# Retention and a squared-ReLU feed-forward in one kernel: q loaded in two DMAs over all partitions, its head groups mixed, and the clusters of small matmuls joined from the fifth group on

## The chip, the cores and the metric

The kernel runs on one core of a Trainium2 chip. Its time is the device time of one execution in microseconds, the median of several runs. A profile is one more execution, recorded by the hardware profiler; its span, 288.5 us here, is counted from the first to the last instruction and is a little shorter than the run's time.

## The reference

Two stages follow each other. The first is retention, attention without a softmax: per head, scores are masked by a decay that falls with distance.

```
scores = (q @ k^T) / sqrt(64)                      # q, k, v: 8 batches, 8 heads, 576 tokens, 64 wide
Dmat   = gamma_h ** (i - j) for i >= j, else 0     # gamma_h = 1 - 2^(-5 - h)
attn   = (scores * Dmat) @ v
x      = attn as (batch, token) rows of 8 x 64 = 512 columns      # 4608 x 512
out    = (relu(x @ w_in) ** 2) @ w_out             # w_in 512 x 2048, w_out 2048 x 512, fp32
```

## The kernel before

**Tiling.** The 4608 tokens are 36 units of 128 tokens: 32 "full" units (a batch, a chunk of 128 tokens) and 4 "tail" units that hold the last 64 tokens of two batches. Two units are a group, so there are 18 groups, numbered from 0 (the fifth is group 4). Retention is done chunk by chunk with a running state R (a 64 x 64 sum of k times v per head, decayed from chunk to chunk); a chunk's output is its own masked scores times v, plus q times the state of the chunks before. The decays are folded into v, into the state and into the output (`gam_full`), so the mask is zeros and ones.

**Where q and k come from.** Both are needed with the 64 columns of a head on the partitions, so they are cast to fp16 and transposed.
- Units 0 to 7 (`PAIRED = 8`) are loaded two at a time, 512 KB each for k, q and v (`add_load_pair`, line 308; the DMA is line 316): a partition holds two neighbouring tokens of every head, in packets of 2 x 64 x 4 = 512 bytes. Casts (line 424, v with its decay line 420) go to VectorE, ScalarE or GpSimd as line 411 says; TensorE transposes (line 439) into a PSUM tile `psT`, and four copies (line 450) bring it to `kqT`. Scores, masks (`mask2`, line 490), state sums and outputs of such a pair are written by `add_ret_pair`; its output becomes `xT` in line 577.
- Units from 8 on are loaded one at a time (`add_load`, line 290). k and v come in packets of 256 bytes, one token of one head. q comes in packets of 1 KB, four tokens of one head, in four DMAs (lines 297 to 299), each to 32 partitions: partition 32 x + r holds tokens 4 r to 4 r + 3 of heads x and 4 + x. GpSimd casts (lines 371, 382, 387) and SyncE's DMA transpose (line 400) makes `kqT`. There the columns of head group x are 32 x to 32 x + 31, so `qT` (line 607) hands the matmuls four runs of 16 neighbouring columns.

**Weights.** w_in and w_out come in four pieces each, issued from GpSimd (line 331), which casts them to fp16 on the way. The first waits for the first v; k of unit 4 waits for the sixth piece (line 318). w_in is used by `ph` (line 876), w_out and four difference matrices wT (line 827) by `po` (lines 916 and 973: from group 1 on the second product is a Strassen scheme with sums gS, line 946).

**Clusters.** Retention's matmuls are 64 x 64 "quads", four at a time on the array, all on line 357. For units from 8 on they stand in clusters: scores and state sums of a group (`fa`, line 778), and its outputs (`fb`, line 809). From the group `JOIN` on, they are joined: `f1` (line 790) is the state part of group g's outputs with group g+1's scores, `f2` (line 794) is group g+1's sums with the rest of g's outputs.

**What sets the order.** Every engine's program is written by a planner (`Schedule`, lines 16 to 100) at build time. A task has an engine, a key (the lowest key of the ready ones goes first), an estimated duration, dependences and buffers that it takes. The planner plays the estimates through and emits the instructions in that order; on the chip each engine then runs its list in order and waits where data are late. Loads, transposes and stores are all on SyncE's list. Junk matmuls (line 256, `WARM = 34` of them) have the last key and fill TensorE's start. VectorE tasks have fixed durations in the planner, whether GpSimd works beside them or not.

Of the kernel before, what the change touches and what calls it, by code (L numbers as in the profile page):

```python
# [15 lines left out]
class Schedule:  # L16
# [6 lines left out]

    def add(self, eng, key, dur, fn, deps=(), acq=(), after=None, lag=0.0):
        t = dict(eng=eng, key=key, dur=dur, fn=fn, acq=acq, n=len(self.tasks), users=[], free=[], lag=lag,
                 left=len(deps), ready=0.0, lat=self.LAT[eng] if after is None else after)
        for d in deps:
            d["users"].append(t)
        self.tasks.append(t)
        return t  # L30
# [11 lines left out]
    def emit(self):  # L42
# [13 lines left out]
        now = 0.0  # L56
        while True:
            for e in ready:
                if busy[e]:
                    continue  # L60
                held = []
                while ready[e]:
                    item = heapq.heappop(ready[e])
                    t = item[2]
                    if all(self.count[r] >= t["acq"].count(r) for r in t["acq"]):
                        for r in t["acq"]:
                            self.count[r] -= 1
                        t["start"] = now
                        order.append(t)
                        busy[e] = True  # L70
                        push(now + t["dur"], "end", t)
                        break
                    held.append(item)
                for item in held:
                    heapq.heappush(ready[e], item)
            if not events:
                break
            now = events[0][0]
            while events and events[0][0] <= now + 1e-9:
                _, _, what, t = heapq.heappop(events)  # L80
                if what == "end":
                    busy[t["eng"]] = False
                    for w in t["users"]:

                        push(now + (0.0 if w["eng"] == t["eng"] else t["lat"]), "dep", w)
                    for g in t["free"]:
                        push(now + t["lat"], "free", g)
                elif what == "dep":
                    t["left"] -= 1
                    if t["left"] == 0:  # L90
                        push(now + t["lag"], "go", t)
                elif what == "go":
                    heapq.heappush(ready[t["eng"]], (t["key"], t["n"], t))
                else:
                    t["left"] -= 1
                    if t["left"] == 0:
                        self.count[t["res"]] += 1
# [6 lines left out]
def kernel(  # L104
# [105 lines left out]

    mask2 = const.tile([P, 2, 2, 64], FP32, name="mask2")
    nc.gpsimd.memset(mask2, 1.0)
    for c in range(2):
        for e in range(2):
            m = mask2[c * 64:(c + 1) * 64, e]
            nc.gpsimd.affine_select(out=m, in_=m, compare_op=ALU.is_ge, fill=0.0, base=-e, pattern=[[1, 2], [2, 64]],  # L216
                                    channel_multiplier=-2)
# [17 lines left out]
    SQ_LATE = (1, 4, 6)  # L235
    JOIN = 5
    LAG = {"k4": 0.7, "q4": 0.5}
    LAG_T, LAG_O = 1.5, 5.0
# [51 lines left out]
    def add_load(u):  # L290
        kind, b, c = units[u]
        for n, (name, src) in enumerate((("k", k), ("q", q), ("v", v))):
            def fn(name=name, src=src):
                x = ld.tile([P, H, D], FP32, name=f"{name}32", tag=f"{name}32")
                tile_of[name + "32", u] = x
                if kind == "full" and name == "q":
                    for j in range(NP):
                        nc.sync.dma_start(out=x[32 * j:32 * j + 32].rearrange("r (a t) d -> r a (t d)", a=2),
                                          in_=src[b, :, c * P:(c + 1) * P, :].rearrange("(a x) (r t) d -> x r a (t d)", a=2, t=4)[j])
                elif kind == "full":  # L300
# [7 lines left out]
    def add_load_pair(name, u):  # L308
        n = "kqv".index(name)

        def fn():
# [91 lines left out]
    def add_unit_pair(u, base):  # L403
# [4 lines left out]
        for i, name in enumerate("kqv"):  # L408
            xs[name] = []
            for e in range(2):  # L410
                eng = ("DVE" if (e if name == "v" else lead) else "ACT" if name == "k" and u >= 4 or u == 2 and e else
                       "DVE" if name == "q" and u == 2 else "POOL")

                def fc(name=name, e=e, eng=eng):
# [4 lines left out]
                    if name == "v":  # L419
                        (nc.vector if eng == "DVE" else nc.gpsimd).tensor_tensor(  # L420
                            out=t.rearrange("p (h d) -> p h d", d=D), in0=x,
                            in1=vdec[f"pair{e}"].rearrange("p (h o) -> p h o", o=1).to_broadcast([P, H, D]), op=ALU.mult)
                    else:
                        engines[eng](out=t.rearrange("p (n b a d) -> p n b a d", n=2, b=2, a=2),
# [9 lines left out]
        for i, name in enumerate("kq"):  # L434
# [9 lines left out]
            for s in range(2):  # L444
                on_act = i == 0 or s == 0 or u > 0

                def fe(i=i, s=s, on_act=on_act):
                    if i == 0:
                        tile_of["kqT", u + s] = work.tile([P, 2 * NP, P], FP16, name="kqT", tag="kqT", bufs=6)
                    (nc.scalar.copy if on_act else nc.vector.tensor_copy)(  # L450
                        out=tile_of["kqT", u + s][:, i * NP:(i + 1) * NP].rearrange("p x (e t) -> p e x t", e=2),
                        in_=tile_of["psT", u, i][:, :, :, half(s)])
                es.append(add("ACT" if on_act else "DVE", base + 3 + i + s / 2, 0.66, fe, deps=[t] + T["kqT", u + s],
# [14 lines left out]
    def add_ret_pair(g):  # L468
# [7 lines left out]
        for e in range(2):  # L476
# [11 lines left out]
            for a in range(2):  # L488
                def fm(e=e, a=a):
                    nc.vector.tensor_tensor(  # L490
                        out=rT[e][:, a], in0=rT["ps", e][a].rearrange("p (n i) -> p n i", i=P),
                        in1=mask2[:, e].rearrange("p (o e) i -> p o (e i)", o=1).to_broadcast([P, NP, P]), op=ALU.mult)
                ms.append(add("DVE", base + 5 + e, 0.66, fm, deps=[t] + ms))
# [79 lines left out]
        for s in range(2):  # L573
            def fx(s=s):
                if s == 0:
                    tile_of["x", g] = x_pool.tile([P, NP, 2 * P], FP16, name="xT", tag="xT")
                nc.vector.tensor_tensor(
                    out=tile_of["x", g][:, :, s * P:(s + 1) * P].rearrange("p n (i e) -> p n e i", e=2),
                    in0=tile_of["psO", g][s].rearrange("p (n e i) -> p n e i", n=NP, e=2),
                    in1=gam_f.rearrange("p n (i e) -> p n e i", e=2), op=ALU.mult)  # L580
            T["x", u + s] = add("DVE", base + 25 + s, 0.7, fx, deps=[t] + ([T["x", u]] if s else []), acq=() if s else ("x",))
# [119 lines left out]
    def after_sums(g, t, key, res):  # L701
# [23 lines left out]
        r1 = add("DVE", key + 0.2 - URGENT, 0.69, fr1, deps=[r0])  # L725
        r2 = add("DVE", key + 0.3, 0.65, fr2, deps=[r1], acq=("R",))
        T["Rm", g], T["R", g], T["Rread", g], T["Rmread", g] = r0, r2, [], r1
# [94 lines left out]
    def add_wT(i, in0, in1):  # L822
        ts = []
        for h in range(2):
            def f(h=h):
                sl = slice(h * HF // 2, (h + 1) * HF // 2)
                nc.vector.tensor_tensor(out=wT[i][:, sl], in0=in0[:, sl], in1=in1[:, sl], op=ALU.subtract)
            ts.append(add("DVE", WT_KEY + i, 0.7, f, deps=sum((wcast[j] for j in range(4, 8 if i else 6)), [])))
        return ts
# [5 lines left out]
    for x, y in ((t2, t1), (t4, t2)):  # L835
        for p in y:
            for w in x:
                sched.need(w, p)
    wT_done = {7: t3, 6: t2, 5: t1, 4: t4}
# [18 lines left out]
    def add_ff(g):  # L858
# [10 lines left out]
        for fb in range(NF // nf):  # L869
# [18 lines left out]
            def fg(fb=fb, on_act=on_act):  # L888
# [43 lines left out]
    def add_strassen(g, us, base, sq):  # L932
# [179 lines left out]
```

## Time and profile before

| what | value |
|---|---|
| time, median of 3 runs | 289.84 us (289.72 to 289.88) |
| span of the profiled run | 288.5 us |
| TensorE busy | 280.7 us, 97% of the span |
| ScalarE busy | 187.5 us, 65% |
| VectorE busy | 177.7 us, 62% |
| GpSimd busy | 87.1 us, 30% |
| ph, line 876 | 1152 matmuls, 136.6 us |
| q loads of units from 8 on | 96 DMAs of 64 KB, median 3.2 us to landing |
| q loads of units 0 to 7 | 4 DMAs of 512 KB, median 6.1 us to landing |

How to read it: a busy TensorE is one with a matmul in its pipeline, so a matmul's listed 273 ns is its latency; a run of 256-column ones goes in one each 109 ns (64 in 6.99 us on the chain of work). The time of a stretch of matmuls is therefore read from the start of one group to the start of the next. Junk matmuls count as busy too. In a time line, brackets at the end of a row hold the idle time of that engine before the row and what ended it. The chain of work that ended last goes back from the last instruction to whatever released it; TensorE has 88% of it, and DMA 3%.

### The profile page before, as it was taken

What the parts mean: (1) busy time and instruction counts of PE and PEld (TensorE: products, weight loads), DVE (VectorE), ACT (ScalarE), POOL (GpSimd) and SP (SyncE); (2) the same over time, 40 slices, a digit from 0 to 9 for tenths busy, and PEclk for the clock granted to TensorE, in tenths of its full rate; (3) what the DMA queues carried; (4) which work ended last, traced back from release to release, by engine and by line L of the source; (5) the groups of instructions that cost most, each with busy time, mean ns of one, the idle gap of its engine ahead of it and who ended that gap; (6) DMA issues with size and microseconds to landing.
All of it is one profiled execution on the core that took longest, in us unless ns stands there. A gap on an engine that the chain in (4) does not pass through costs nothing.

```text
span 288.5 us, 10135 instructions
## 1 busy us (share of the span) xinstructions
PE 280.7 (97%) x4346; PEld 236.0 (82%) x4346; DVE 177.7 (62%) x341; ACT 187.5 (65%) x363; POOL 87.1 (30%) x124
## 2 busy tenths in 40 slices
PE   7999999999999999999999999999999999999994
PEld 2568767888888888888888888888888888888883
DVE  3772389868466756657666574767666566364632
ACT  5558975667584757667575748675848665847830
POOL 5660045433525243423325151534433100000000
PEclk9999999999999999999999999999999999999999
DMA  7999999999999898989898997989899420102004
GB/s 202 275 208 206 248 277 267 168 240 144 212 222 186 210 201 216 179 214 168 222 146 197 231 185 182 220 200 248 177 160 228 110 75 5 73 2 75 0 2 145
DMA packets 122156, 49.94 MB, mean 173 GB/s; under 512 B 94720, under 2 KB 117760, under 8 KB 122112
## 3 DMA queue, kind: packets, MB, share of 16 engines
q1 hardware_dynamic: 117568, 44.84, 71.0%
q0 software_dynamic: 4224, 4.19, 8.8%
q8 instruction: 34, 0.56, 0.8%
q10 hardware_dynamic: 320, 0.26, 0.4%
q14 instruction: 10, 0.08, 0.1%
HBM read 36.70 MB, written 9.44 MB: 160 GB/s over the span
## 4 chain that ended last, share of the span: by engine, by line
PE 88%; DMA 3%; DVE 3%; POOL 2%; issue 2%; DVEq 0%; POOLq 0%
PE ph L876 43%; PE po L973 36%; PE psO L357 4%; DMA w_in<-in_moe_w_in_dram 3%; PE po L916 2%; PE psS L357 2%; PE psc L357 2%; DVE rx L490 1%; DVE o L996 1%; DVE gS L946 1%; POOL mask L216 0%; DVE vx L420 0%; POOL vx L420 0%; POOL w_in L331 0%; PE psT L439 0%
## 5 line engine op out<-in xcount | busy, mean ns | idle before, releaser
L876 PE MATMUL ph<-xT,w_in 128*128 128x256 f16 x1152 | 136.6, 273 | 0.3 <-DMA w_in<-in_moe_w_in_dram 0.3
L876 PEld LDWEIGHTS <-w_in 128*128 128x128 f16 x1152 | 111.4, 98 | 14.7 <-DMA w_in<-in_moe_w_in_dram 0.6
L884 ACT ACTIVATE rl<-ph 128x512 f16<-128x512 f32 x144 | 84.3, 586 | 50.7 <-PE ph L876 48.1
L894 ACT ACTIVATE gT<-rl 128x512 f16<-128x512 f16 x118 | 74.4, 631 | 3.4
L973 PEld LDWEIGHTS <-gS 128*128 128x128 f16 x544 | 51.7, 98 | 6.5
L973 PE MATMUL po<-wT,gS 128*128 128x256 f16 x408 | 55.8, 273 | 0.0
L946 DVE TENSOR_TENSOR gS<-gT,gS 128x512 f16<-128x512 f16 (+1 forms) x51 | 31.3, 613 | 24.2 <-ACT gT L894 23.7
L973 PEld LDWEIGHTS <-gT 128*128 128x128 f16 x408 | 39.6, 98 | 4.8
L973 PE MATMUL po<-w_out,gT 128*128 128x256 f16 x272 | 36.8, 273 | 0.0
L387 POOL TENSOR_TENSOR v<-v,vdec_full 128x512 f16<-128x512 f32 x24 | 26.6, 1108 | 28.1 <-DMA v<-in_v_dram 24.4
L371 POOL CAST kq<-k 128x512 f16<-128x512 f32 x28 | 19.7, 702 | 36.9 <-DMA k<-in_k_dram 31.2
L946 DVE TENSOR_TENSOR gS<-gT 128x1024 f16<-128x1024 f16 x34 | 24.7, 726 | 6.4 <-ACT gT L894 6.3
L382 POOL CAST kq<-q 128x512 f16<-128x512 f32 x24 | 15.6, 649 | 32.0 <-DMA q<-in_q_dram 31.8
L896 DVE TENSOR_TENSOR gT<-rl 128x512 f16<-128x512 f16 x26 | 11.8, 455 | 20.1 <-ACT rl L884 20.1
L996 DVE TENSOR_TENSOR o<-po,u 128x256 f32<-128x256 f32 x33 | 13.9, 422 | 15.3 <-PE po L973 7.7
L986 ACT COPY u<-po 128x256 f32<-128x256 f32 x34 | 12.5, 368 | 15.7 <-PE po L973 15.5
L751 DVE TENSOR_TENSOR xT<-psO,gam_full 128x512 f16<-128x512 f32 x28 | 18.0, 685 | 3.8 <-PE psO L357 3.6
L996 DVE TENSOR_TENSOR o<-po,p 128x256 f32<-128x256 f32 x18 | 7.6, 424 | 20.6 <-ACT u L986 12.7
L973 PE MATMUL po<-w_out,gS 128*128 128x256 f16 x136 | 18.0, 273 | 0.0
L692 DVE TENSOR_TENSOR rT<-psc,mask_full 128x512 f16<-128x512 f32 x24 | 15.6, 685 | 3.7 <-PE psc L357 3.2
L973 PE MATMUL po<-wT,gT 128*128 128x256 f16 x136 | 17.6, 273 | 0.0
L1047 ACT COPY o<-po 128x256 f32<-128x256 f32 x16 | 5.9, 370 | 10.8 <-PE po L973 9.1
(82 smaller groups left out, 227.1 us busy)
## 6 DMA issues: line engine op xcount, KB each, us to landing
out_dram<-o SPq DMA_DIRECT2D x32, 256.0 KB, 3.0
k<-in_k_dram SPq DMA_DIRECT2D x24, 256.0 KB, 4.5
q<-in_q_dram SPq DMA_DIRECT2D x96, 64.0 KB, 3.2
v<-in_v_dram SPq DMA_DIRECT2D x24, 256.0 KB, 3.5
pair<-in_k_dram SPq DMA_DIRECT2D x4, 512.0 KB, 7.0
pair<-in_q_dram SPq DMA_DIRECT2D x4, 512.0 KB, 6.1
pair<-in_v_dram SPq DMA_DIRECT2D x4, 512.0 KB, 6.6
w_in<-in_moe_w_in_dram POOLq DMA_DIRECT2D x4, 512.0 KB, 9.2
```

The costliest lines, as they stand in the source:

```text
L357: t = nc.tensor.matmul(out_, lhsT=lhsT, rhs=rhs, start=start, stop=True, skip_group_check=True, tile_position=(64 * row, 64 * col))
L371: op(out=out_.rearrange("p (n b a d) -> p n b a d", n=2, b=2, a=2), in_=in_.rearrange("p (a n b) d -> p n b a d", n=2, a=2))
L382: nc.gpsimd.tensor_copy(out=tile_of["kq", u][:, 1].rearrange("p (t a d) -> p a t d", t=4, a=2), in_=tile_of["q32", u].rearrange("p (a t) d ...
L387: nc.gpsimd.tensor_tensor(out=t, in0=tile_of["v32", u], in1=vdec[kind].rearrange("p (h o) -> p h o", o=1).to_broadcast([P, H, D]), op=ALU. ...
L692: tile_of["masking", g] = nc.vector.tensor_tensor(out=tile_of["rT", g][:, :, a], in0=tile_of["psc", g][a].rearrange("p (s n i) -> p s n i" ...
L751: nc.vector.tensor_tensor(out=tile_of["x", g].rearrange("p n (s e i) -> p e (n s) i", s=n, e=2)[:, c], in0=y.rearrange("p (o t r) -> p o r ...
L876: nc.tensor.matmul(tile_of["ph", g, fb][:, j, :], lhsT=w_in16[:, m, fi * P:(fi + 1) * P], rhs=tile_of["x", g][:, m, :], start=(m == 0), st ...
L884: nc.scalar.activation(out=t, in_=tile_of["ph", g, fb], func=ACTF.Relu)
L894: nc.scalar.activation(out=t, in_=rl, func=ACTF.Square)
L946: nc.vector.tensor_tensor(out=tile_of["S", g][:, k, sl], in0=in0(sl), in1=in1(sl), op=op)
L973: nc.tensor.matmul(tile_of["pb", g, bank], lhsT=left(i), rhs=right[:, i, :], start=(start and i == 0), stop=(i == HF - 1), skip_group_chec ...
L996: nc.vector.tensor_tensor(out=o_tile(u)[:, half * HM:(half + 1) * HM], in0=bank(x), in1=tile_of[name, g], op=ALU.add)
```

## The change

q is laid out otherwise. For units from 8 on, one DMA takes four heads over all 128 partitions: partition 4 r + x holds tokens 4 r to 4 r + 3 of heads x and 4 + x. Two DMAs do what four did, with the same packets. The head groups are then mixed: the columns of head group x in `kqT` are x, x + 4, x + 8 and so on, and `qT` steps by four. The paired units get the same layout with eight tokens to a packet, so 2 KB in place of 512 bytes; `mask2`, the q eviction and line 577 follow its order of tokens.

The rest is about order. Clusters are joined from group 4 (`JOIN = 4`); casts of units from group 5 on get an earlier key with it. The planner learns that a VectorE task marked `soft` (two SBUF inputs) runs at 0.22 of its speed while GpSimd has a task of over 0.5 us. Squares on VectorE, sums and one ReLU of group 1 are hurried by 60 keys; the halves of wT wait only for the pieces they read; junk matmuls go from 34 to 26; casts of k and q of unit 2 all go to ScalarE; estimated durations and lags are set anew.

The diff, cut to its core (the hunks of the planner's class are its model of shared speed and are left out):

```
...
-    mask2 = const.tile([P, 2, 2, 64], FP32, name="mask2")
+    mask2 = const.tile([P, 2, 8, 16], FP32, name="mask2")
...
-            nc.gpsimd.affine_select(out=m, in_=m, compare_op=ALU.is_ge, fill=0.0, base=-e, pattern=[[1, 2], [2, 64]],
+            nc.gpsimd.affine_select(out=m, in_=m, compare_op=ALU.is_ge, fill=0.0, base=-e, pattern=[[1, 8], [8, 16]],
...
-    WARM = 34
+    WARM = 26
...
-    BESIDE = 1.1
+    HURRY = 60
...
-    JOIN = 5
-    LAG = {"k4": 0.7, "q4": 0.5}
+    JOIN = 4
+    LAG = {"k0": 0.3, "w7": 1.4, "v6": 1.2}
...
-                    for j in range(NP):
-                        nc.sync.dma_start(out=x[32 * j:32 * j + 32].rearrange("r (a t) d -> r a (t d)", a=2),
-                                          in_=src[b, :, c * P:(c + 1) * P, :].rearrange("(a x) (r t) d -> x r a (t d)", a=2, t=4)[j])
+                    for a in range(2):
+                        nc.sync.dma_start(out=x[:, NP * a:NP * a + NP].rearrange("p t d -> p (t d)"),
+                                          in_=src[b, :, c * P:(c + 1) * P, :].rearrange("(a x) (r t) d -> a r x (t d)", a=2, t=4)[a])
...
-            t = nc.sync.dma_start(out=x, in_=(k, q, v)[n][b, :, c * P:(c + 2) * P, :].rearrange("h (p e) d -> p h (e d)", e=2))
+            src = (k, q, v)[n][b, :, c * P:(c + 2) * P, :]
+            if name == "q":
+                for a in range(2):
+                    t = nc.sync.dma_start(out=x[:, NP * a:NP * a + NP].rearrange("p t d -> p (t d)"),
+                                          in_=src.rearrange("(a x) (r t) d -> a r x (t d)", a=2, t=8)[a])
+            else:
+                t = nc.sync.dma_start(out=x, in_=src.rearrange("h (p e) d -> p h (e d)", e=2))
...
-        loaded[name, u] = loaded[name, u + 1] = dma_task(0, 1.81 if loaded else 2.9, fn, acq=("wst",) if name != "q" else (),
+        loaded[name, u] = loaded[name, u + 1] = dma_task(0, 2.9 if not loaded else 1.41 if name == "q" else 1.81, fn, acq=("wst",) if name != "q" else (),
...
-        t = add("SP", 0, 2.75, lambda: None, deps=last_load + [issue], after=2.1 + LAG.get(f"w{i}", 0.0))
+        t = add("SP", 0, 2.58, lambda: None, deps=last_load + [issue], after=3.0 + LAG.get(f"w{i}", 0.0))
...
-                eng = ("DVE" if (e if name == "v" else lead) else "ACT" if name == "k" and u >= 4 or u == 2 and e else
-                       "DVE" if name == "q" and u == 2 else "POOL")
+                eng = ("DVE" if (e if name == "v" else lead) else "ACT" if name == "k" and u >= 4 or u == 2 and name != "v" else "POOL")
...
+                    elif name == "q":
+                        x = tile_of["q32", u].rearrange("p (a t) (s d) -> p a (t s) d", a=2, s=2)[:, :, NP * e:NP * e + NP]
+                        engines[eng](out=t.rearrange("p (t a d) -> p a t d", t=NP, a=2), in_=x)
...
+                        out_ = out_.rearrange("p x (t r) -> p t x r", r=16)
+                        in_ = in_.rearrange("p e y (r x) -> p (e y) x r", x=NP)[:, :, :, 16 * s:16 * s + 16]
...
-                    out=tile_of["x", g][:, :, s * P:(s + 1) * P].rearrange("p n (i e) -> p n e i", e=2),
-                    in0=tile_of["psO", g][s].rearrange("p (n e i) -> p n e i", n=NP, e=2),
+                    out=tile_of["x", g][:, :, s * P:(s + 1) * P].rearrange("p n (r t) -> p n r t", t=8),
+                    in0=tile_of["psO", g][s].rearrange("p (n t r) -> p n r t", n=NP, t=8),
...
-        return t[:, x, half(c)] if units[u][0] == "tail" else t[:, :, 32 * x + 16 * c:32 * x + 16 * c + 16]
+        return t[:, x, half(c)] if units[u][0] == "tail" else t[:, :, 64 * c + x:64 * c + 64:NP]
...
-            ts.append(add("DVE", WT_KEY + i, 0.7, f, deps=sum((wcast[j] for j in range(4, 8 if i else 6)), [])))
+            ts.append(add("DVE", WT_KEY + i, 0.68, f, deps=wcast[4 + h] + (wcast[6 + h] if i else []), soft=True))
...
-            r = add("ACT", place(4 * fb + 4), 0.6, fr, deps=[f1[-1]], acq=("rl",))
+            r = add("ACT", place(4 * fb + 4) - HURRY * (g == 1 and fb == 7), 0.6, fr, deps=[f1[-1]], acq=("rl",))
...
-            sq.append(add("ACT" if on_act else "DVE", place(4 * fb + 6), 0.63 if on_act else 0.55, fg, deps=[r] + sq[:1],
-                          acq=() if fb else ("g",)))
+            sq.append(add("ACT" if on_act else "DVE", place(4 * fb + 6) - HURRY * (g == 1 and not on_act), 0.63 if on_act else 0.43, fg, deps=[r] + sq[:1],
+                          acq=() if fb else ("g",), soft=not on_act))
...
-                out_.append(add("DVE", key + h, (BESIDE if h else 0.5) if parts > 1 else 0.8, f, deps=deps(h, parts) + list(start)))
+                out_.append(add("DVE", key + h - HURRY * (g == 1), 0.43 if parts > 1 else 0.72, f, deps=deps(h, parts) + list(start), soft=True))
...
```

More of the change, by code (lines that the diff above doesn't have):

```diff
@@ L22, in __init__, with add @@
         self.tasks = []
-    def add(self, eng, key, dur, fn, deps=(), acq=(), after=None, lag=0.0):
-        t = dict(eng=eng, key=key, dur=dur, fn=fn, acq=acq, n=len(self.tasks), users=[], free=[], lag=lag,
+    SHARED = 0.22
+    def add(self, eng, key, dur, fn, deps=(), acq=(), after=None, lag=0.0, soft=False):
+        t = dict(soft=soft, eng=eng, key=key, dur=dur, fn=fn, acq=acq, n=len(self.tasks), users=[], free=[], lag=lag,
                  left=len(deps), ready=0.0, lat=self.LAT[eng] if after is None else after)
@@ L56, in emit, with shared @@
         now = 0.0
+        port = dict(task=None, left=0.0, at=0.0, beside=False)
+        def shared(beside):
+            t = port["task"]
+            if t is not None:
+                port["left"] -= (now - port["at"]) * (self.SHARED if port["beside"] else 1.0)
+                port["at"] = now
+                t["end"] = now + max(port["left"], 0.0) / (self.SHARED if beside else 1.0)
+                push(t["end"], "end", t)
+            port["beside"] = beside
         while True:
@@ L70, in emit @@
                         busy[e] = True
-                        push(now + t["dur"], "end", t)
+                        t["end"] = now + t["dur"]
+                        if t["soft"]:
+                            port.update(task=t, left=t["dur"], at=now)
+                            shared(port["beside"])
+                        else:
+                            push(t["end"], "end", t)
+                        if e == "POOL" and t["dur"] > 0.5:
+                            shared(True)
                         break
@@ L81, in emit @@
                 if what == "end":
+                    if abs(t["end"] - now) > 1e-6:
+                        continue
+                    t["end"] = -1.0
                     busy[t["eng"]] = False
+                    if t["soft"]:
+                        port["task"] = None
+                    elif t["eng"] == "POOL" and t["dur"] > 0.5:
+                        shared(False)
                     for w in t["users"]:
@@ L315, in fn @@
             b, c = units[u][1:]
-            t = nc.sync.dma_start(out=x, in_=(k, q, v)[n][b, :, c * P:(c + 2) * P, :].rearrange("h (p e) d -> p h (e d)", e=2))
+            src = (k, q, v)[n][b, :, c * P:(c + 2) * P, :]
[3 more added lines that the diff above has]
+                                          in_=src.rearrange("(a x) (r t) d -> a r x (t d)", a=2, t=8)[a])
+            else:
+                t = nc.sync.dma_start(out=x, in_=src.rearrange("h (p e) d -> p h (e d)", e=2))
             if (name, u) == ("k", 4):
@@ L449, in fe @@
                         tile_of["kqT", u + s] = work.tile([P, 2 * NP, P], FP16, name="kqT", tag="kqT", bufs=6)
-                    (nc.scalar.copy if on_act else nc.vector.tensor_copy)(
-                        out=tile_of["kqT", u + s][:, i * NP:(i + 1) * NP].rearrange("p x (e t) -> p e x t", e=2),
-                        in_=tile_of["psT", u, i][:, :, :, half(s)])
+                    out_, in_ = tile_of["kqT", u + s][:, i * NP:(i + 1) * NP], tile_of["psT", u, i]
+                    if i == 0:
+                        out_, in_ = out_.rearrange("p x (e t) -> p e x t", e=2), in_[:, :, :, half(s)]
+                    else:
+                        out_ = out_.rearrange("p x (t r) -> p t x r", r=16)
+                        in_ = in_.rearrange("p e y (r x) -> p (e y) x r", x=NP)[:, :, :, 16 * s:16 * s + 16]
+                    (nc.scalar.copy if on_act else nc.vector.tensor_copy)(out=out_, in_=in_)
                 es.append(add("ACT" if on_act else "DVE", base + 3 + i + s / 2, 0.66, fe, deps=[t] + T["kqT", u + s],
@@ L491, in fm @@
                         out=rT[e][:, a], in0=rT["ps", e][a].rearrange("p (n i) -> p n i", i=P),
-                        in1=mask2[:, e].rearrange("p (o e) i -> p o (e i)", o=1).to_broadcast([P, NP, P]), op=ALU.mult)
+                        in1=mask2[:, e].rearrange("p (o t) r -> p o (t r)", o=1).to_broadcast([P, NP, P]), op=ALU.mult)
                 ms.append(add("DVE", base + 5 + e, 0.66, fm, deps=[t] + ms))
@@ L577, in fx @@
                 nc.vector.tensor_tensor(
-                    out=tile_of["x", g][:, :, s * P:(s + 1) * P].rearrange("p n (i e) -> p n e i", e=2),
-                    in0=tile_of["psO", g][s].rearrange("p (n e i) -> p n e i", n=NP, e=2),
-                    in1=gam_f.rearrange("p n (i e) -> p n e i", e=2), op=ALU.mult)
+                    out=tile_of["x", g][:, :, s * P:(s + 1) * P].rearrange("p n (r t) -> p n r t", t=8),
+                    in0=tile_of["psO", g][s].rearrange("p (n t r) -> p n r t", n=NP, t=8),
+                    in1=gam_f.rearrange("p n (r t) -> p n r t", t=8), op=ALU.mult)
             T["x", u + s] = add("DVE", base + 25 + s, 0.7, fx, deps=[t] + ([T["x", u]] if s else []), acq=() if s else ("x",))
@@ L725, in after_sums @@
         r1 = add("DVE", key + 0.2 - URGENT, 0.69, fr1, deps=[r0])
-        r2 = add("DVE", key + 0.3, 0.65, fr2, deps=[r1], acq=("R",))
+        r2 = add("DVE", key + 0.3, 0.62, fr2, deps=[r1], acq=("R",), soft=True)
         T["Rm", g], T["R", g], T["Rread", g], T["Rmread", g] = r0, r2, [], r1
@@ L835 @@
     for x, y in ((t2, t1), (t4, t2)):
-        for p in y:
-            for w in x:
-                sched.need(w, p)
+        for w, p in zip(x, y):
+            sched.need(w, p)
     wT_done = {7: t3, 6: t2, 5: t1, 4: t4}
```

## The prediction

> **What bounds the kernel now.** I read first the slices of the page, then a table of windows, then the chain of work that ended last, then the time line around its weak places. The slices say which engine is full and when.
>
> ```profile
> PE   7999999999999999999999999999999999999994
> DMA  7999999999999898989898997989899420102004
> ```
>
> TensorE is full from the second slice to the last but one, but its first slices hold junk matmuls (line 256), so "busy" there is not work. The windows show where it is not full (columns: stretch, its length, each engine's busy us and count, clock, DMA share, GB/s).
>
> ```profile
> 18.00:20.00 2.00, 1.68 (x17) 1.26 (x15) 2.00 (x5) 1.16 (x3) 1.31 (x2) 1.00 1.24 206
> 20.00:40.00 20.00, 19.90 (x191) 14.64 (x192) 8.22 (x15) 17.43 (x32) 0.95 (x2) 1.00 1.22 239
> 40.00:52.00 12.00, 11.61 (x256) 9.20 (x254) 10.84 (x18) 7.02 (x15) 6.69 (x8) 1.00 0.93 248
> 86.00:260.00 174.00, 173.90 (x2932) 152.09 (x2932) 109.47 (x189) 115.15 (x223) 52.95 (x65) 1.00 0.78 168
> ```
>
> From 86 to 260 us TensorE idles 0.10 of 174 us: nothing that makes another engine or a load faster is worth anything there. Idle that can be won lies at 18 to 20 (0.32) and at 40 to 52 (0.39, with VectorE busy 10.84 of 12). The rest of the possible gain is the junk before the first real feed-forward matmul. The time line shows what that one waits for.
>
> ```profile
> 16.02 1.04 PE L256 MATMUL warm<-wT 128*128 128x512 f16 x4
> 16.98 0.81 PE L357 MATMUL psc<-kqT 64*64 64x128 f16 x32
> 17.73 1.92 PE L876 MATMUL ph<-xT,w_in 128*128 128x256 f16 x16
> 19.97 0.28 PE L876 MATMUL ph<-xT,w_in 128*128 128x256 f16 x1 [0.33 <-DMA w_in<-in_moe_w_in_dram]
> ```
>
> The first group's xT is ready at 15.95 (line 577, started 14.60, two of some 0.68), yet ph starts at 17.73 and stops again until 19.97 for the second piece of w_in. The chain has the same wait.
>
> ```profile
> 10.94 8.99 DMA w_in<-in_moe_w_in_dram
> 19.93 0.05 issue
> ```
>
> So the start is paced by bytes: DMA share over 1 all along, and the weights stand behind six 512 KB loads of the first four units. How fast those run is seen where casts waited for them, and how fast the weights run where line 827 waited for the sixth piece.
>
> ```profile
> 10.42 0.62 ACT L424 CAST kx<-pair 128x512 f16<-128x512 f32 x1 [1.63 <-DMA pair<-in_k_dram]
> 12.24 0.62 ACT L424 CAST qx<-pair 128x512 f16<-128x512 f32 x1 [1.20 <-DMA pair<-in_q_dram]
> 13.99 0.69 DVE L420 TENSOR_TENSOR vx<-pair,vdec_pair 128x512 f16<-128x512 f32 x1 [0.29 <-DMA pair<-in_v_dram]
> 30.12 0.69 DVE L827 TENSOR_TENSOR wT<-w_out 128x1024 f16<-128x1024 f16 x1 [0.71 <-DMA w_out<-in_moe_w_out_dram]
> ```
>
> k, q, v of units 2 and 3 land 1.82 and 1.75 us apart: 1.79 us per 512 KB in packets of 512 B. Weight pieces 1 to 5 land between 19.97 and 30.12, 10.15 / 4 = 2.54 us per 1 MB of fp32 read in runs of 2 KB: 1.27 us per 512 KB.
>
> **What the Trainium skill says.** DMA: Bandwidth & Descriptors, Specifications, asks for 512 B or more per packet for line rate, and its section Why small descriptors are slow adds a fixed 3 cycles of the internal bus per packet. By that, 512 B costs 16 + 3 cycles and four of them 76, a 2 KB packet 64 + 3 = 67: 12% less, an estimate of 0.21 us per 512 KB. The trace's two rates differ by 0.52 us; the measurement decides, but the weights are written at half width, so I keep both ends.
> SBUF — State Buffer, SBUF: two separate sides and its cacheline note: a 16-byte line must be hit twice for full rate. A q column every four fp16 elements is 8 bytes, two hits per line: just free. No trace here shows a TensorE operand read so.
> The same page, Who interferes with whom: a VectorE operation with two SBUF inputs and a GpSimd operation that reads SBUF lock each other out. The trace agrees: line 896 has a median of 424 ns and a maximum of 830. The planner now reckons with it.
> TensorE: Matmul & The Clock Gate, Part 1: about 3.4 us of idle lets the clock halve. The longest gap on TensorE before 20 us is 1.26 us and the granted clock is 1.00.
>
> **The change part by part.**
> 1. *q of the paired units, 512 B to 2 KB packets.* Two q loads stand ahead of the first weights. Saving each: between 0.21 (the page) and 0.52 (trace); the planner's own figures go from 1.81 to 1.41. I take 0.45, nearer the trace: 2 x 0.45 = 0.9 us for all weights. The split into two DMAs adds one issue of some 0.45 us on SyncE per load (v of line 301 takes 0.43); behind it waits v0, whose bytes have k0 and q0, 1 MB, ahead of them, so it hides. Weight piece 1 then lands at 19.1. xT of group 0 was ready 1.78 us before it was used, so it doesn't take over; group 1's scores wait on q2, which comes about 0.9 earlier too. **-0.9 us.**
> 2. *Fewer junk matmuls (34 to 26).* Eight at 0.216 = 1.73 us; four of them fill the 0.9 us that disappear, the others leave gaps well under 3.4 us. **0.**
> 3. *Casts of units 2 and 3 all on ScalarE.* Four of 0.62 in place of two; ScalarE idled 1.63 and 1.20 us ahead of its two casts. It frees VectorE of 0.42 and takes GpSimd's cast (11.75, behind the weight issues) out of the way. Gain inside item 1.
> 4. *The q eviction (line 450) reads PSUM in steps of four, and xT (line 577) in steps of 16.* For xT, line 751 already reads that way at 685 ns against 728: no cost. The eviction on ScalarE should stay near 0.53; the one on VectorE (0.425, unit 0) may fall to the 0.68 of its other PSUM reads, +0.26, inside the 1.78 us of slack. **0.**
> 5. *Units 4 to 7, and the VectorE order at 40 to 52 us* (the hurried squares and sums of group 1, first halves of wT released earlier, the shared-port model). Their loads come 0.9 earlier from the weights and 0.45 or 0.9 more from their own q. TensorE idles 0.39 us here, 0.31 of it for a line-420 product that VectorE runs late. I take most of it: **-0.3 us** (0 to -0.4).
> 6. *Joining from group 4.* Now group 4's outputs stand alone (gap between big matmuls from 66.11 + 16 x 0.1092 = 67.86 to 68.86: 1.00 us) and so do group 5's scores and sums (76.34 + 8 x 0.1092 = 77.21 to 77.98: 0.77). A joined pair is seen at 85.85 to 86.45 (0.60) and 89.95 to 90.83 (0.88). 1.77 - 1.48 = **-0.3 us**. It needs group 5's q and k some 10 us earlier than now. SyncE, which is issuing nearly without a break, sets that:
>
> ```profile
> 45.07 1.90 SPq L298 DMA_DIRECT2D q<-in_q_dram x4
> 47.01 0.43 SPq L301 DMA_DIRECT2D v<-in_v_dram  x1
> ```
>
> Two q issues fewer per unit save about 0.95 us; by unit 11 that is four units, 3.8 us, and with items 1 and 5 nearly 6. Its transposes, issued at 64.17 and 67.83 with 4.3 us to landing, would then be in by about 66; group 4's outputs went at 67.95. Group 4's first ph is needed only when group 3's 64 end, at 75.6, so a late cluster costs nothing: 5 us of ph stand before it.
> 7. *q of the other 24 units in two DMAs.* 24 x 0.95 = 23 us of SyncE, packets unchanged at 1 KB. After 86 us TensorE waits for no load, so **0** beyond item 6.
> 8. *Strided q in the matmuls.* 24 units, 16 score quads each, and 16 with the state less 8 for each of six first chunks: 384 + 336 = 720. 32 quads take 0.27 us (62.38 to 62.65), 8.4 ns each. Free: 0. At half rate: 720 x 8.4 = +6.0 us, all on TensorE and so all on the path. I take **0**, with 6.0 as the other end.
>
> Sum: -0.9 - 0.3 - 0.3 = -1.5, so 289.84 becomes **288.3 us**.
>
> **The rivals.**
> - *Only a part arrives* (15%): the packet gain is the page's 0.21 twice, the bubbles stay, the join is eaten by a masking wait: -0.4 or so, 289.4. For it: the page calls 512 B enough. Against: 1.79 against 1.27.
> - *More arrives* (9%): the packet gain is the full 0.52 twice, and ph starts without its second stop (0.32), with items 5 and 6 whole: -1.04 - 0.32 - 0.7, about 287.7; with VectorE less blocked by GpSimd at 40 to 72 us, down to 287.0.
> - *Strided columns cost* (8%): 288.3 + 6.0 = 294.3 at half rate, 291.3 at three quarters. For it: two hits per line is the very limit. Against: the page's rule.
> - *The new order opens a hole, slower* (8%): group 5's loads are late, the joined cluster stands at the head of TensorE's order, and what is queued behind it, ph and products, waits some 2 to 3 us once: 288.3 + 2.5 = 290.8. For it: DMA share is 1.05 between 68 and 86. Against: 5 us of slack at 75.6.
>
> **How the numbers follow.** My forecast has 60%. It and the greater gain lie below the 0.2% bound of 289.26; of the first rival about half does. Faster: 60 + 9 + 6 = 75%. Same: the other 9%. Slower: 16%. The range runs from 287.1 (unknown sizes of items 1 and 5) to 289.8 (nothing arrives); it leaves out the two slower rivals and the tip of the greater gain, some 18%.
>
> **What would show it.** The q cast of unit 2 should start by 11.4 rather than 12.24, the first ph by 16.9, ph's second stop end by 19.2. The q load's line should count 48 issues. The cluster at 77.31 should be gone, with group 5's scores beside psO near 67. Line 357's 32 score quads should still take 0.27 us: 0.5 would prove the strided read costly. I'm wrong if the weights land no earlier though q does, if ph of group 0 starts on xT and not on w_in, or if a TensorE gap of over a microsecond appears between 60 and 80 us.

## The result, and the profile after

The changed kernel takes 294.99 us (median of 4 runs, 294.56 to 295.13) against 289.86 (4 runs): a ratio of 1.0174, 95% interval 1.0156 to 1.0191. It is slower by some 5 us, where 1.5 us less was forecast.

The slices of the page after look like those of before: TensorE is full.

```profile
PE   8879999999999999999999999999999999999994
DMA  7999999999998999999787978779946010201004
```

The windows say the same of the idle time (columns as before: stretch, length, busy us and count of each engine, clock, DMA share, GB/s).

```profile
18.00:20.00 2.00, 2.00 (x20) 1.79 (x19) 1.97 (x5) 1.01 (x2) 0.68 (x1) 1.00 1.23 205
20.00:40.00 20.00, 19.61 (x200) 14.62 (x198) 8.58 (x17) 18.58 (x34) 1.17 (x2) 1.00 1.21 248
40.00:52.00 12.00, 11.46 (x241) 8.39 (x240) 11.19 (x19) 5.92 (x13) 8.03 (x9) 1.00 1.07 263
86.00:260.00 174.00, 173.86 (x2850) 151.13 (x2848) 106.19 (x184) 114.87 (x221) 50.80 (x62) 1.00 0.75 162
```

From 86 to 260 us TensorE idles 0.14 of 174 us, but it starts 2850 matmuls there instead of 2932: it is as full as before and gets less done. So no wait has been added in this stretch; some matmuls have become longer. Which ones is seen in the views by tile. Of `kqT`, which holds k and q after the transpose, first in the kernel after, then before (columns after the count: shortest, median, longest in ns).

```profile
L390 PE MATMUL psc<-kqT x576: 189/234/240, 10.0 to 244.0; 64*64 64x64 f16 x149, 64*64 64x128 f16 x43
L390 PE MATMUL psO<-kqT,Rm x192: 215/231/242, 72.5 to 251.2; 64*64 64x64 f16 x192
```

```profile
L357 PE MATMUL psc<-kqT x576: 192/193/240, 9.0 to 238.8; 64*64 64x64 f16 x149, 64*64 64x128 f16 x43
L357 PE MATMUL psO<-kqT,Rm x192: 186/193/213, 68.0 to 244.2; 64*64 64x64 f16 x192
```

The quads that read q in steps of four went from 193 to 231 or 234 ns. The score quads of the tail units, whose q stays in neighbouring columns, did not: of the 448 score quads with 64 columns the 384 of full units took over 210 ns, the other 64 didn't. These are latencies; the time the quads hold the array is read from start to start. Group 4's cluster in the time line after:

```profile
62.84 0.65 PE L390 MATMUL psc<-kqT 64*64 64x64 f16 x32
63.31 0.46 PE L390 MATMUL psS<-v,kq 64*64 64x64 f16 x32
63.70 0.50 PE L914 MATMUL ph<-xT,w_in 128*128 128x256 f16 x3
```

32 score quads now take 63.31 - 62.84 = 0.47 us where they took 0.27; the 32 state sums behind them, which don't read q, take 0.39 (0.40 before). Taking all clusters of small matmuls together, and counting for each the time from the end of the last big matmul's slot (its start + 0.1092) to the next big start, the trace before has 29.0 us in them and the trace after 34.4: 5.4 us more. From the first ph to the last po it is 266.4 us before (17.73 to 284.09) and 271.6 after (17.88 to 289.44): 5.2 more. The clusters hold the whole loss.

### The profile page after: what moved, and what is told of

The parts are those of the page before. It is cut to its first block, busy times and chain, and to the rows that moved or that the text cites. A ratio compares the mean times of both kernels' runs of the same rounds, so it can differ in the third digit from the quotient of the medians.

```text
span 293.4 us, 10054 instructions
## 1 busy us (share of the span) xinstructions
PE 284.7 (97%) x4338; PEld 239.1 (82%) x4338; DVE 178.4 (61%) x340; ACT 188.9 (64%) x365; POOL 86.3 (29%) x123
## 4 chain that ended last, share of the span: by engine, by line
PE 85%; DMA 10%; DVE 2%; POOL 1%; SPq 1%; issue 1%; ACT 0%; DVEq 0%; POOLq 0%
PE ph L914 39%; PE po L1011 36%; DMA pair<-in_v_dram 5%; DMA w_out<-in_moe_w_out_dram 5%; PE psO L390 5%; PE psc L390 3%; PE psS L390 2%; POOL vx L452 1%; DVE rx L529 1%; PE po L954 1%; SPq L346 0%; PE psT L474 0%; DVE o L1034 0%; POOL w_in L364 0%; POOL w_out L364 0%
## 5 line engine op out<-in xcount | busy, mean ns | idle before, releaser
L1011 PE MATMUL po<-wT,gS 128*128 128x256 f16 x408 | 54.8, 273 | 0.0
L420 POOL TENSOR_TENSOR v<-v,vdec_full 128x512 f16<-128x512 f32 x24 | 25.7, 1073 | 20.8 <-DMA v<-in_v_dram 13.7
L984 DVE TENSOR_TENSOR gS<-gT 128x1024 f16<-128x1024 f16 x34 | 25.6, 753 | 6.3 <-ACT gT L932 5.1
L415 POOL CAST kq<-q 128x512 f16<-128x512 f32 x24 | 17.3, 722 | 36.7 <-DMA q<-in_q_dram 36.4
L934 DVE TENSOR_TENSOR gT<-rl 128x512 f16<-128x512 f16 x26 | 12.4, 479 | 16.6 <-ACT rl L922 16.6
L390 PE MATMUL psc<-kqT 64*64 64x64 f16 (+1 forms) x576 | 12.5, 226 | 1.2 <-issue 1.0
```

The costliest lines, as they stand in the source:

```text
L390: t = nc.tensor.matmul(out_, lhsT=lhsT, rhs=rhs, start=start, stop=True, skip_group_check=True, tile_position=(64 * row, 64 * col))
L415: nc.gpsimd.tensor_copy(out=tile_of["kq", u][:, 1].rearrange("p (t a d) -> p a t d", t=4, a=2), in_=tile_of["q32", u].rearrange("p (a t) d ...
L420: nc.gpsimd.tensor_tensor(out=t, in0=tile_of["v32", u], in1=vdec[kind].rearrange("p (h o) -> p h o", o=1).to_broadcast([P, H, D]), op=ALU. ...
L1011: nc.tensor.matmul(tile_of["pb", g, bank], lhsT=left(i), rhs=right[:, i, :], start=(start and i == 0), stop=(i == HF - 1), skip_group_chec ...
```

## The experiments

**1. The changed kernel, q read in neighbouring columns.** Its instruction lists are those of the changed kernel on every engine; only the columns that the quads read differ.

```
-        return t[:, x, half(c)] if ... else t[:, :, 64 * c + x:64 * c + 64:NP]
+        return t[:, x, half(c)] if ... else t[:, :, 32 * x + 16 * c:32 * x + 16 * c + 16]
```

> The changed kernel with one edit: the matmuls of units from 8 on read q in four runs of 16 neighbouring columns, as before, though the load still mixes the head groups. So heads get each other's q columns and the output differs from the reference; instructions, sizes, loads and order are those of the changed kernel. Theory (the read in steps of four columns is the loss): 32 score quads go back from 0.47 to 0.27 us, 720 quads lose some 6 ns each and the time falls by 4 to 5.5 us, to about 290. Rival (the loss is in the new order, the joined group 4 or the loads): the time stays within 1 us of 295.

Measured: 289.71 us, a ratio to before of 0.9969 (0.9953 to 0.9985). The cluster of above in this kernel:

```profile
62.70 0.45 PE L390 MATMUL psc<-kqT 64*64 64x64 f16 x32
62.98 0.46 PE L390 MATMUL psS<-v,kq 64*64 64x64 f16 x32
63.37 0.61 PE L914 MATMUL ph<-xT,w_in 128*128 128x256 f16 x4
```

0.28 us for the 32 quads, and the last po starts at 284.54 instead of 289.44. All clusters together: 29.9 us against 34.4, so 4.5 us / 720 quads = 6.2 ns each. Another 0.27 us of the 4.9 between the two profiled runs is a later first ph (17.88 against 17.61). The medians lie 5.3 us apart (294.99 and 289.71, from different sessions of runs). The strided read is the loss. The 0.9 us that the clusters still have over those of before (29.9 against 29.0) is not the read's. Without the strided read the rest of the change makes the kernel faster by 0.3% against the kernel before in the same session (median 290.55); against the 289.86 of the result it is 0.05%, and the two profiled spans are equal, 288.5 us.

**2. The kernel before, q read in steps of four.** The same edit the other way round, in the order and with the loads of before.

> The kernel before with one edit: the matmuls of units from 8 on read q in steps of four columns from the layout of before, so heads get each other's q columns and the output differs from the reference. Loads, order and everything else are those of before. Theory (the strided read is the loss): 289.9 + 4 to 5.5, about 294.5, with 32 score quads at 0.47 us. Rival (order, join or loads): no change, 289.9 within 0.6.

Measured: 294.50 us, ratio 1.0128 (1.0091 to 1.0165): 3.7 us more (2.6 to 4.8) than the kernel before in the same session, 4.6 more than 289.86. In the profiled runs the clusters grow by 4.6 us as well, from 29.0 to 33.7. The 32 quads of group 4:

```profile
61.81 0.65 PE L357 MATMUL psc<-kqT 64*64 64x64 f16 x32
62.27 0.46 PE L357 MATMUL psS<-v,kq 64*64 64x64 f16 x32
```

0.46 us. Read alone, the step makes the loss in either kernel.

**3 and 4. Steps of two and of eight columns**, in the changed kernel: `64 * c + x:64 * c + x + 32:2` and `4 * c + x:128:8`.

> The changed kernel with q read in steps of two columns instead of four (heads get other columns, so the output differs from the reference). Two readings of the loss in the kernel with steps of four: (A) it goes with the number of 16-byte lines that a run touches, so steps of two, half the lines, cost little or nothing: 32 score quads in 0.27 to 0.3 us and a time near 290 to 291. (B) any step over one costs the same: 0.47 us and 295.

> The changed kernel with q read in steps of eight columns, 16 bytes (heads get other columns, so the output differs from the reference). (A) a line for every column, twice the lines of steps of four: 32 score quads take about 0.9 us and the time rises by 8 to 10 us over 295, to about 304. (B) any step over one costs the same: 0.47 us and 295.

Measured in one run each: 290.24 and 305.28 us, the second a little more than forecast. Group 4's clusters, steps of two first:

```profile
62.77 0.47 PE L390 MATMUL psc<-kqT 64*64 64x64 f16 x32
63.07 0.45 PE L390 MATMUL psS<-v,kq 64*64 64x64 f16 x32
```

```profile
62.45 1.10 PE L390 MATMUL psc<-kqT 64*64 64x64 f16 x32
63.37 0.47 PE L390 MATMUL psS<-v,kq 64*64 64x64 f16 x32
```

So 32 quads take 0.28, 0.30, 0.47 and 0.92 us at steps of 1, 2, 4 and 8. A quad's 64 columns (four runs of 16, each column 2 bytes) then touch 8, 16 to 20, 32 and 64 lines of 16 bytes, the line that the prediction reckoned with. Per quad that is 8.8, 9.4, 14.7 and 28.8 ns; the last two are 0.46 and 0.45 ns a line. Reading (A) fits and (B) doesn't: with four quads side by side, a quad takes the longer of some 9 ns and 0.45 ns for each line. Whether it is the lines that count or the bytes that a run spans is not told apart, since the two grow together at these steps. Steps of two are all but free, steps of four are not.

**5. The changed kernel with q loaded in four DMAs and unmixed** (the load and the read of before, everything else changed).

> The changed kernel with q of units from 8 on loaded in four DMAs of 32 partitions and read in neighbouring columns, as before; the paired units, the join from group 4 and the new order stay. Theory (strided read): as the kernel with the mixed load and the contiguous read, about 290 and within 0.6 of it, since after 86 us no engine waits on SyncE's issues. Rival A (the two-DMA load is worth something by itself): over 1 us slower than that one. Rival B (order or join is the loss): still about 295.

Measured: 293.12 us, ratio 1.0081 (1.0050 to 1.0112). Rival A's number, and my 290 missed. The quads are short again (psc 193 ns), but three joined clusters wait. The longest:

```profile
123.08 0.32 PE L390 MATMUL psO<-kqT,R 64*64 64x64 f16 x16
123.22 0.30 PE L390 MATMUL psc<-kqT 64*64 64x64 f16 x16
125.18 0.32 PE L390 MATMUL psc<-kqT 64*64 64x64 f16 x16 [1.66 <-DMA kqT<-kq]
```

The scores of one unit are there, those of the second wait 1.66 us for its transpose. The planner had put the joined cluster where two-DMA loads are in time: with them, in experiment 1, the cluster at this place of the same list takes 0.60 us, here 2.45. That TensorE waits for no load after 86 us was true of the order of before, not of this one.

**6. The changed kernel with the join from group 5** (`JOIN = 5`, strided read kept).

> The changed kernel with clusters joined from group 5, as before. Strided-read theory: the join itself is worth little, 295.0 within 0.6; by the clusters' gaps in the trace (0.91 + 0.97 joined against some 1.1 + 0.95 apart) 0.2 slower. Rival (the join from group 4 opened a hole): 2 us or more faster.

Measured: 294.94 us, ratio 1.0140 (1.0109 to 1.0171). No difference from 294.99: the join made no hole, and no gain.

**7. Unmixed, and the join from group 5** (experiments 5 and 6 together, with the contiguous read).

> The changed kernel with q of units from 8 on loaded in four DMAs and read in neighbouring columns, and with the join from group 5: what stays of the change is the paired units' q in 2 KB packets and the planner's new order. If the 3.4 us between the unmixed kernel (293.1) and the mixed load with a contiguous read (289.7) come from the early join meeting late loads, the three clusters that waited on transposes there (2.45, 1.40 and 0.97 us where 0.60 is usual) go back to 0.60 and the time is about 290. If the four-DMA load costs by itself, it stays at 292 to 293.

Measured: 291.23 us median, ratio 1.0040 (1.0025 to 1.0055), single runs from 289.82. The profiled run, one of 289.82, has all its joined clusters at 0.60; the others were not profiled. The early join accounts for a part of the 3.4 us, not for all of it.

**8. The same, unit 0's second q eviction on ScalarE.**

```
-                on_act = i == 0 or s == 0 or u > 0
+                on_act = True
```

> As the unmixed kernel with the join from group 5, and unit 0's second q eviction on ScalarE in place of VectorE, where it stands behind a product that waits for v0 (row at 9.77 us). If that wait is why the first feed-forward matmul starts at 17.88 though the first weights land at 16.08, ph starts about 0.5 us earlier, its second stop on the second weights (19.18) comes back in part, and the time falls by 0.3 to 0.5 us. Rival (the start is paced by something else): no change within 0.2.

Measured: 291.23 us, ratio 1.0043 (1.0020 to 1.0066): no change. ph started at 17.09 us instead of 17.35 and the scores of unit 0 at 9.58 instead of 9.78; the time didn't follow. That the eviction held up the start by 0.26 us is only a hint: the changed kernel and that of experiment 4 have the same lists, and in their profiled runs ph started at 17.88 and 17.35. By the profile two joined clusters (82.50 and 121.74) took 1.13 and 1.46 us instead of 0.60, which hides so small a gain.

**9. Before, with the paired units' q in 2 KB packets only.**

> The kernel before with one part of the change: the paired units' q in two DMAs of 2 KB packets, with the casts, eviction, mask and xT that follow from it. Order, loads of the other units and the join from group 5 are those of before. The prediction's item 1 says 0.9 us faster, 288.9. Theory now: the second weight piece lands some 0.7 us earlier, but k of unit 4 waits for the sixth piece, which did not land earlier in the changed kernel, so 0.2 to 0.5 us faster, about 289.5. Rival: VectorE's slower eviction (0.68) and q0's later landing eat it, no change.

Measured: 289.94 us, ratio 0.9984 (0.9971 to 0.9997): faster by 0.1 to 0.8 us, some 0.5. Of the kernels here that change nothing of what is computed it is the only one whose interval lies below the kernel before. Its profiled run, one of 290.50 us, does not show the gain.

**10. Before, with q in two DMAs, read contiguously.**

```
-                    for j in range(NP):
-                        nc.sync.dma_start(out=x[32 * j:32 * j + 32]...
+                    for a in range(2):
+                        nc.sync.dma_start(out=x[:, NP * a:NP * a + NP]...
```

> The kernel before with one part of the change: q of units from 8 on in two DMAs over all partitions, head groups mixed, while the matmuls still read neighbouring columns (heads get each other's q columns, so the output differs from the reference). Theory: SyncE's 23 us of issues are off the path in the order of before, so 289.9 within 0.4. Rival (the four issues cost something of themselves, as the 3.4 us of the unmixed kernel might mean): over 0.6 us faster than before.

Measured: 289.61 us, ratio 0.9978 (0.9968 to 0.9989): faster by 0.3 to 0.9 us. The theory, nothing within 0.4, is at the edge, and the rival's bound of 0.6 lies in the interval. In the one profiled run TensorE starts its 275th matmul of ph and po (30 us of them at 0.1092) at 59.37 us, at 59.88 before, and keeps that half microsecond to the end. Where the gain comes from in runs without a profile is not shown. In part it is a lack of late runs: the 22 runs reach up to 290.53 us, those of the kernel before in the same session up to 292.17 (one at 294.72 is not counted).

**11. Contiguous, two DMAs, the join from group 5.**

> The changed kernel with the contiguous read (other heads' columns, so the output differs from the reference) and the join from group 5. Against the same with the join from group 4 (289.7) it gives the join's worth without the strided read. Prediction: 0.3 slower, 290.0. Rival: no difference, as with the strided read (294.9 against 295.0).

Measured: 289.91 us, ratio 0.9987 (0.9978 to 0.9997), against 0.9969 (0.9953 to 0.9985) with the join from group 4. The ratios differ by 0.5 us and the medians by 0.2, both the way of the forecast 0.3, but the intervals overlap: not settled.

**12. All q loaded and read as before, in the new order**, join from group 5: the paired units' layout is undone too.

> The changed kernel's order with every q loaded and read as before: paired units in 512 B packets, the others in four DMAs, join from group 5. What is left of the change is the planner's new order, lags and casts. Against the unmixed kernel with the join from group 5 (291.2, where single clusters wait on late transposes) it gives the 2 KB packets' worth in the new order: 0.5 to 0.9 slower if the new order counts on them. Rival: the same 291.2, because the wait for transposes sets the time.

Measured: 292.89 us, ratio 1.0116 (1.0075 to 1.0158), 1.7 us slower than experiment 7 and more than the 0.5 to 0.9 expected. That the new order counts on the 2 KB packets fits this, but is not shown: in the profiled run the 18th matmul of ph starts at 21.17 us (19.21 in experiment 7), and most of this comes with the clock (columns as before).

```profile
14.00:17.00 3.00, 1.90 (x102) 1.46 (x101) 2.58 (x5) 1.54 (x4) 2.67 (x3) 1.00 1.24 207
18.00:20.00 2.00, 2.00 (x13) 1.45 (x11) 1.97 (x5) 0.12 (x1) 1.50 (x3) 0.50 1.24 206
```

The granted clock is 0.50, and the first 14 matmuls of ph take 2.88 us where 14 x 0.1092 = 1.53 would do: some 1.35 us, an estimate. No other profiled run here has this between 8 and 280 us. The clock isn't the whole loss: one of the six runs, with a mean clock of 1.00, took 292.63 us. One joined cluster (122.52) takes 1.58 us in the profiled run.

## Why the prediction was wrong

**The step that failed is item 8**, strided q in the matmuls. I counted the quads rightly (720), read 8.4 ns each from the profile, bounded the cost at 0 and 6.0 us, and then took 0. The Trainium skill, SBUF — State Buffer, section SBUF: two separate sides, asks for at least two hits in a 16-byte line for full bandwidth, and I took two as enough. A step of four fp16 columns gives just two hits. The trace had no such read, and the rival that "two hits per line is the very limit" got 8%. Experiments 1 to 4 show 14.7 ns in place of 8.8: +5.9 ns x 720 = 4.3 us, or 4.5 summed over the clusters (5.3 between the medians). Page and measurement differ, and the measurement decides: for TensorE's moving operand two hits are not enough, four are. That the rival's 294.3 came near the outcome is partly luck: it has 6.0 for the read, where 4.5 to 5.3 was measured, and -1.5 for the rest, where experiment 1 has -0.9 (-0.4 to -1.4).

**Item 1, the packets: the landing was right, what it is worth was not.** The second weight piece landed at 19.18 (19.93 before), as forecast (19.1). The way there was another: the q load of unit 2 took 1.46 us after k's landing, not 1.79, a saving of 0.33 where I took 0.45; but q0 took 2.20 and landed later than before (7.27 against 6.78), so the two loads together were no sooner in. How the weights came to be 0.75 earlier is open. ph should have started by 16.9 but did at 17.88. The chain of the kernel after shows a part of the reason: VectorE runs unit 0's eviction after the product with v0, and waits for v0 first.

```profile
2.68 6.39 DMA pair<-in_v_dram
9.07 0.03 issue
9.09 0.02 DVEq L452
9.12 0.04 issue
9.16 0.69 DVE vx L452
9.85 0.61 DVE kqT L491
10.46 0.04 issue
10.50 0.46 PE psc L390 x15
```

Then group 1's scores stand in TensorE's list ahead of ph:

```profile
16.11 0.61 PE L390 MATMUL psc<-kqT 64*64 64x128 f16 x29
17.70 0.25 PE L390 MATMUL psc<-kqT 64*64 64x128 f16 x3 [0.98 <-issue]
17.88 3.23 PE L914 MATMUL ph<-xT,w_in 128*128 128x256 f16 x28
```

For the 0.98 us ahead of the last three the profile names no releaser, so the cause stays open. It was not the weights: the first piece had landed at 16.08 us, while xT of group 0 was done at 17.03, 1.08 later than before. Nor did the weights set this start in the kernel before by more than some 0.15 us, though the prediction read it so: there the first piece landed at 17.43, the last scores of group 1 started at 17.58 and ph at 17.73, and in experiment 9, where it landed at 15.59, ph started at 17.95. In every profiled run here ph starts 0.14 to 0.25 us after the last of these scores. So earlier weights could give little more than ph's second stop (0.33).

ph has no second stop any more, and its first 28 matmuls end at 17.88 + 28 x 0.1092 = 20.94, before at 19.97 + 12 x 0.1092 = 21.28. So 0.34 of the 0.9 us reached TensorE. Even that was lost at 30 us, where po of group 0 waits for the sixth weight piece, which lands no earlier than the 30.10 of before:

```profile
16.43 13.80 DMA w_out<-in_moe_w_out_dram
30.23 0.04 issue
30.27 1.02 PE po L954 x4
```

The ph ahead of it ended its slots at 28.23 + 16 x 0.1092 = 29.98, so TensorE stops for 0.29 us. k of unit 4, which waits for the same piece, was issued at 30.29 us (30.25 before). By itself, in the order of before, the item is worth some 0.5 us (experiment 9).

**Item 2** held in the changed kernel: the granted clock is 1.00 in every window from 18 us on. But the bound behind it, that gaps stay well under 3.4 us, is no guard: in experiment 12, with the same 26 junk matmuls, the clock fell to 0.50 though TensorE's longest gap after its first 2 us was 1.01. **Item 3** moved the casts as planned, but its sign failed: the q cast of unit 2 started at 12.33, not by 11.4, since q2 landed at 12.25.

**Item 4**: sizes right. VectorE's eviction took 0.68 us and ScalarE's stayed at 592 ns; the xT product (line 577, now 616) took a median of 680 ns, less than the 730 of before. That 1.78 us of slack hid the eviction is doubtful, with xT done 1.08 us later and the hint of 0.26 us in experiment 8.

**Item 5** failed: TensorE idles 0.54 us at 40 to 52 instead of 0.39. The loads of units 4 to 7 came earlier (v of unit 4 at 39.93 against 40.66), but the clusters of these units stood earlier in the list as well (the state sums of unit 4 behind 158 matmuls of ph and po instead of 178).

**Item 6**: nothing measurable. The joined cluster of group 4 came at 72.5, not 67. I had two q issues save 0.95 us per unit: a two-DMA issue takes a median of 604 ns each, so 1.25 with its gaps against 1.90, and 0.65 is saved. For four units that makes 1.2 of the 3 us by which group 5's second transpose landed later than forecast (69.00 against 66). The cluster stands another 3.5 us behind that in the planner's list; why is not shown. It opened no hole in the changed kernel, as the slack at 75.6 said. Its gain of 0.3 is neither shown nor refuted (experiments 6 and 11).

**Item 7**, 0 for two DMAs, was a little too low: 0.3 to 0.9 us faster in the order of before. In the new order they are needed (experiments 5 and 7 against 1 and 11).

## What to carry to other kernels

A layout that saves issues or packets on a queue with slack must not be paid for on the engine that is full: here some 16 us of queue time (24 units x 0.65) and at most about a microsecond of gain stood against 6 ns on 720 small matmuls, and the small matmuls won. When a strided operand of the bounding engine shows up in no trace and its two ends lie 6 us apart while the rest of the change is worth 1.5, measure that operand first, or forecast the range, not the rule. And an order planned for faster loads is part of the change: undoing the loads alone (experiment 5) gave a third kernel, slower than the one before by 0.8%.

## What the runs showed of the hardware

- TensorE's moving operand from SBUF, fp16, 64 rows, four 64 x 64 quads side by side: steps of 1 and 2 columns cost nearly the same (8.8 and 9.4 ns a quad), steps of 4 and 8 cost 14.7 and 28.8, which is 0.45 ns for each 16 bytes spanned. Two hits to a 16-byte line are not enough for full rate there.
- The loss shows in no wait and no idle time: only in the latency of the quads (193 to 234 ns) and in the distance from one start to the next.
- A copy of 512 fp16 columns from PSUM that reads in steps of four and writes runs of 16 took VectorE 681 ns where the one with runs of 64 took 425 (one copy each); ScalarE's had a median of 592 in both (15 copies each).
- Half the DMAs, each with twice the packets (128 of 1 KB to 128 partitions in place of 64 to 32), made an issue of 604 ns out of one of 430: SyncE's cost per load fell by a third, not by half.
- In one profiled run (experiment 12) the granted clock fell from 1.00 to 0.50 between 17.3 and 20.8 us, with TensorE busy for 1.90 of the 3 us before and no gap over 1.01 us after its first 2 us.
